# Query transposes moved ahead of the first up, three scans behind it, and three small sums moved later, in a fused linear-attention and SoLU kernel

## The chip, the cores and the metric

One core of a Trainium2 chip runs the whole program in one launch. The metric is the device time of one execution in microseconds (us); for the kernel before, the median of 3 runs is 367.84 (367.70 to 368.34). TensorE is called PE here, its weight loads PEld, VectorE DVE, ScalarE ACT, GpSimd POOL, and the engine that issues most of the transfers SP.

## What is computed

The reference, cut to what matters (4 batches, 8 heads, 768 steps, head width 48; 3072 tokens, model width 384, hidden width 1024; float32):

```python
state = zeros((B, H, D, D))
for t in range(S):
    state = alpha[:, :, t, :, None] * state + einsum('bhd,bhe->bhde', k[:, :, t], v[:, :, t])
    y[:, :, t] = einsum('bhd,bhde->bhe', q[:, :, t], state)
x = y.transpose(0, 2, 1, 3).reshape(B * S, H * D)
h = x @ w_in
solu = h * softmax(h)
ln = (solu - mean(solu)) / sqrt(var(solu) + 1e-6) * g_ln
return ln @ w_out
```

So each head carries a 48 by 48 state, decayed per row by alpha, and the attention's output goes through a hidden layer with a softmax gate and a layer norm.

## The kernel before, in words

**Tiling.** The 768 steps are cut into 6 groups of 128 steps; a group holds 128 steps of all 4 batches, 512 tokens, that is 4 output tiles of 128 tokens. Groups are counted from 0 in the code: g or a = 2 is the third. For each group there are two halves of work:

- *Attention.* Decays, keys and queries are turned so that the head's rows lie on partitions. `alpha_T` (L187) turns alpha by two DVE transposes (`firsts` L178, 128x1024, and `lasts` L181, 128x512). `scan_back` (L206) makes products of decays from each step to the group's end (`hT`), three parts; `inverses` (L211) takes a reciprocal; `scan_on` (L215) makes the products from the start (`aT`), again three parts of 128x516, part 2 for the last 16 rows of the heads and parts 0 and 1 for the first 32 rows. All six scans are DVE instructions of L204. `keys_T` and `keys` (L219, L223) turn the keys on DVE and multiply them on POOL (L225). `queries(i)` (L250, L253) multiplies part i of the queries by `aT` on POOL; `apart` (L243, L245, ACT) splits the last rows by parity. `scores` (L271, L278) multiplies keys and queries on PE into four banks, `masked` (L286, L289, DVE) takes them to `sT`; `read_state` and `read_values` (L348, L356, L333) make the output x; `next_state` (L365) carries the state. `move_lasts` and `move_firsts` (L227, L234) copy the queries within the on-chip memory by twelve transfers from SP's queue into `lot`, from which `decay` (L255, L261, POOL) and `read_state` read.
- *Hidden layer.* For each of 8 slices s of the hidden width, `up` (L386) makes h on PE (6 matmuls, L394) in one of two banks, ACT takes the exponent `e` (L408), DVE the product `room` (L409), ACT its square (L412). `room` frees the bank of h. `running` (L415, L427) adds the slices up in p, one half on POOL, one on DVE. `token_sums` (L454) adds up over partitions on PE (L462), transposes the result on DVE (L467) and makes from it, by three small DVE operations (L469, L471, L473), what `finish` needs. `down` (L501, L507) makes an output tile on PE, `finish` (L518) scales it: small DVE operations, a power on POOL (L546), ACT (L548), the transfer out (L549).

**Order.** The order on each engine is that of the code; nothing is rearranged. The first two groups' attention and the first group's hidden layer are written out by hand (L668 to L843). From L922 on a loop runs over groups g = 1 to 5, with steps s = 0 to 7: at each step comes one `up` of group g, and pieces of group g+1's attention are hung in by a table, `first` (L853) for g = 1 and `usual` (L847) for the others. Places of a step are, in order: head, up, behind, `running`, middle, `down`, tail. In `first`, step 1 has "on1" behind the up (one scan of the third group), step 2 "lasts firsts" (query transposes, POOL's products and the moves), step 3 `keys_back` at its head and "apart" behind, steps 4 and 5 the scores and masks. In `usual`, step 1 has all three scans. With g = 1 no `down` is in the loop's steps 0 to 6, so that PE goes from one up to the next.

By hand, in front of the loop, stand for the third group: `alpha_T(2)` (L818), `scan_back(2, .)` (L836), `inverses(2)`, `keys_T(2)`, `keys(2)`, the loads of alpha and keys of the fourth group (L834, L840) and `scan_on(2, 2)`, `scan_on(2, 0)` (L842, L843). The load of the fourth group's queries is issued by "firsts" in step 2 (L888), behind the moves in SP's queue. SP waits at each transfer that it issues until its sources and its target are free.

Of the kernel before, what the change touches and what calls it, by code (L numbers as in the profile page):

```python
# [9 lines left out]
FP = mybir.dt.float32  # L10
# [4 lines left out]
ALU = mybir.AluOpType  # L15
AX = mybir.AxisListType
P = 128
# [15 lines left out]
def fast_path(ctx, tc, q, k, v, alpha, moe_w_in, moe_w_out, moe_g_ln, out):  # L33
# [12 lines left out]
    nc = tc.nc  # L46
    B, H, S, D = q.shape
    NTOK, DM = out.shape
    DFF = moe_w_in.shape[1]
# [12 lines left out]
    def pool(name, bufs, **kw):  # L62
        return ctx.enter_context(tc.tile_pool(name=name, bufs=bufs, **kw))
# [4 lines left out]
    small = pool("small", 4)  # L68
# [31 lines left out]
    qn = const.tile([P, H, TQ, D], FP, name="qn")  # L100
# [20 lines left out]
    qv = const.tile([P, 2 * H, SW], FP, name="qv")  # L121
    qe = const.tile([P, NP, SW], FP, name="qe")
# [5 lines left out]
    gr = [dict() for _ in range(G)]  # L128


    def load(src, dst, g):
        t = slice(g * P, (g + 1) * P)
        for b in range(B):
            nc.sync.dma_start(
                out=dst[32 * b : 32 * b + 32].rearrange("t h u d -> t h (u d)"),
                in_=src[b, :, t, :].rearrange("h (t u) d -> t h (u d)", u=TQ),
            )
# [35 lines left out]
    def load_v(g):  # L173
        t = slice(g * P, (g + 1) * P)
        for b in range(B):
            nc.sync.dma_start(out=held(vn, b), in_=v[b, :, t, :].rearrange("h p d -> p h d"))

    def firsts(src, dst):  # L178
        nc.vector.transpose(out=dst.rearrange("p h (t u) -> p h u t", u=TQ), in_=src[:, :, :, 0:E0])  # L179

    def lasts(src, dst):  # L181
        nc.vector.transpose(
            out=dst.rearrange("p j (i t u) -> p u j i t", u=TQ, i=2),
            in_=src[:, :, :, E0:D].rearrange("p (j i) u d -> p u j i d", i=2),
        )
# [14 lines left out]
    def scan(out, data, start, flip):  # L200
        a, o, s = (x.rearrange("p j s -> p (j s)") for x in (data, out, start))
        if flip:
            a, o, s = a[:, ::-1], o[:, ::-1], s[:, ::-1]
        nc.vector.tensor_tensor_scan(out=o, data0=a, data1=s, initial=1.0, op0=ALU.mult, op1=ALU.add)  # L204
# [10 lines left out]
    def scan_on(g, i):  # L215
        part = slice(NP * i, NP * i + NP)
        scan(aT[:, part], aT[:, part], seed[:, part], False)

    def keys_T(g):  # L219
        firsts(kn, kT[:, 0:H])  # L220
        lasts(kn, kT[:, H:NB])
# [43 lines left out]
    def quarter(b):  # L265
        return slice(32 * b, 32 * b + 32)
# [19 lines left out]
    def masked(half, batches=range(B)):  # L286
        a = masks[half]
        for b in batches:
            nc.vector.tensor_tensor(  # L289
                out=sT[:, b, half * NP : half * NP + NP], in0=a[b], in1=mask[:, None, :].to_broadcast([P, NP, P]),  # L290
                op=ALU.mult,
            )
# [161 lines left out]
    def token_sums(g):  # L454


        d = gr[g]
        t = ps_a.tile([P, B, 2, 32], FP, tag="a3", name="rows") if g else ps_h.tile([P, B, 2, 32], FP, tag="h", name="rows")
        for b in range(B):
            for r in range(4):  # L460
                c = b * P + 32 * r
                nc.tensor.matmul(  # L462
                    t[quarter(r), b], lhsT=d["unit"][:, 0:32], rhs=d["p"][:, :, c : c + 32], start=True, stop=True,
                    tile_position=(0, 32 * r), skip_group_check=True,
                )
        tt = work.tile([P, B, 2, 32], FP, name="cols")
        nc.vector.transpose(out=tt.rearrange("p b i t -> p (b i t)"), in_=t.rearrange("p b i t -> p (b i t)"))  # L467
        s = sums[:, g * B : g * B + B]
        nc.vector.tensor_copy(out=s[:, :, 1:3], in_=tt[:, :, :, 0])  # L469
        sq = small.tile([P, B], FP, name="sq")  # L470
        nc.vector.tensor_tensor(out=sq, in0=s[:, :, 1], in1=s[:, :, 1], op=ALU.mult)  # L471
        d["s"] = small.tile([P, B], FP, name="s")
        nc.vector.scalar_tensor_tensor(  # L473
            out=d["s"], in0=sq, scalar=1e-6 * DFF, in1=s[:, :, 2], op0=ALU.mult, op1=ALU.add
        )

    def last_norm():

# [39 lines left out]
    def finish(n):  # L518
        g, b = divmod(n, B)
        d = st[n]  # L520
        s, whole = sums[:, n], d.get("held", d["o"])
        o = whole[:, 0:DM]
        t0 = b * S + g * P
        if g == G - 1:
            o_sb = work.tile([P, DM], FP, name="o_sb")
            r = gr[g]["r"][:, b : b + 1]
            nc.vector.tensor_scalar(out=o_sb[:, 0:P], in0=o[:, 0:P], scalar1=r, scalar2=None, op0=ALU.mult)  # L527
            nc.scalar.activation(out=o_sb[:, P:DM], in_=o[:, P:DM], func=AF.Copy, scale=r)  # L528
            nc.scalar.dma_start(out=out[t0 : t0 + P, :], in_=o_sb)
            d.clear()  # L530
            return
        nc.vector.tensor_copy(out=s[:, 0:1], in_=whole[:, DM : DM + 1])
        t = small.tile([P, 1], FP, name="t")
        nc.vector.scalar_tensor_tensor(
            out=t, in0=s[:, 0:1], scalar=-1.0 / DFF, in1=s[:, 0:1], op0=ALU.mult, op1=ALU.mult
        )
        nc.vector.tensor_tensor(out=s[:, 3:4], in0=t, in1=gr[g]["s"][:, b : b + 1], op=ALU.add)  # L537
        if g == 0:

            centred = work.tile([P, DM], FP, name="o_mean")  # L540
            nc.vector.scalar_tensor_tensor(
                out=centred, in0=mean_sb, scalar=s[:, 0:1], in1=o, op0=ALU.mult, op1=ALU.add
            )
            o = centred
        r = small.tile([P, 1], FP, name="r")
        nc.gpsimd.tensor_tensor(out=r, in0=s[:, 3:4], in1=mhalf, op=ALU.pow)  # L546
        o_sb = work.tile([P, DM], FP, name="o_sb")
        nc.scalar.activation(out=o_sb, in_=o, func=AF.Copy, scale=r)  # L548
        nc.sync.dma_start(out=out[t0 : t0 + P, :], in_=o_sb)  # L549
        d.clear()  # L550
# [166 lines left out]
    for i in (0, 2, 1):  # L717
        if i == 1:
# [3 lines left out]
            out=qe[:, :, 0:P] if i == 2 else qv[:, part, 0:P], in0=t[i], in1=aT[:, part, 1:SW], op=ALU.mult  # L722
# [98 lines left out]
    down(2, 1)  # L821
    scores(1, 1)
    masked(1)
    finish(0)
    finish(1)
    finish(2)
# [8 lines left out]
    for i in range(3):  # L835
# [3 lines left out]
    keys(2)  # L839
    load(k, kn, 3)  # L840
    down(3, 1, (2, 3))
    scan_on(2, 2)  # L842
    scan_on(2, 0)  # L843

# [6 lines left out]
    first = dict(  # L853
        head={3: "keys_back"},
        behind={
            0: "v", 1: "on1", 2: "lasts firsts", 3: "apart", 4: "scores0 masked0", 5: "scores1 masked1 decay",
            7: "alpha back",
        },
        tail={6: "begin read0"},
# [3 lines left out]
    def attend(a, what):  # L863

        more = a + 1 < G
        if what == "v":
            load_v(a)
        elif what == "keys":
            keys_T(a)
            keys(a)  # L870
            if more:
                load(k, kn, a + 1)
        elif what[:2] == "on":
            if what == "on2":
                inverses(a)
            scan_on(a, int(what[2]))
        elif what == "lasts":
            lasts(qn, qe[:, :, 0:P])
            ends_of_decay()
            queries(2)  # L880
            move_lasts()
        elif what == "firsts":
            firsts(qn, qv[:, 0:H, 0:P])
            queries(0)
            queries(1)
            move_firsts()
            if more:
                load(q, qn, a + 1)  # L888
        elif what == "apart":
            apart()  # L890
        elif what == "decay":
            decay(a)
        elif what == "keys_back":
            if more:
                keys_back(a)
        elif what[:6] == "scores":
            scores(a, int(what[6]))
        elif what[:6] == "masked":
            masked(int(what[6]))
        elif what == "alpha" and more:  # L900
            alpha_T(a + 1)
            if a > 2:
                attend(a, "over")
        elif what == "over" and more:
            alpha_over(a + 1)
            if a + 2 < G:
                load(alpha, an, a + 2)
        elif what == "back" and more:
            for i in range(3):
                scan_back(a + 1, i)  # L910
        elif what == "begin":
            read_begin()
        elif what[:4] == "read":
            read_state(int(what[4]))
        elif what == "values":
            read_values(a)
        elif what == "kv" and more and a != 4:
            next_state(a)
# [59 lines left out]
    def compare(out, x, bound, op):  # L978
# [6 lines left out]
        out=chunks[:, :, 2], in0=sums[:, :, 2], scalar=0.25, in1=sums[:, :, 3], op0=ALU.mult, op1=ALU.is_le  # L985
# [6 lines left out]
    else:  # L992
# [9 lines left out]
        out=bad, in0=all_ok[0:1, 0:1], scalar1=float(P * ends[-1]), scalar2=None, op0=ALU.is_lt  # L1002
# [451 lines left out]
```

## Time and profile before

| what | value |
|---|---|
| median of 3 runs | 367.84 us |
| the profiled execution's own time | 367.97 us |
| span of the profiled execution | 366.2 us |
| TensorE clock granted | 1.0 of full speed |
| DVE scans, L204 | 36, mean 1399 ns (`hT`) and 1551 ns (`aT`) |
| DVE transposes of the queries, 128x1024 and 128x512 | mean 2032 and 1107 ns |
| L469, L471, L473 on DVE | mean 172, 166 and 166 ns |
| POOL key product L225, 128x1024 | mean 2182 ns |
| POOL query products L253 | mean 1090 (`qe`) and 1240 ns (`qv`) |

The profile is of one execution. Its page gives busy time by engine and groups of instructions by line; the timeline gives the start and length of each instruction, counted from the span's start, with the idle time before it and what ended that; `out<-in` names the tiles. "x4" merges instructions in a row. Ends of matmuls are modelled, so lengths of PE's rows overlap the next row; starts don't. A wait is put down to what came last.

### The profile page before, as it was taken

The page shows a single profiled execution, that of the slowest core. Times are in us where ns is not written, and L with a number is a line of the kernel's source. Part 1 is how long each engine was busy: PE and PEld are TensorE (multiplying, and loading weights), DVE is VectorE, ACT ScalarE, POOL GpSimd, SP SyncE. Part 2 cuts the span into 40 slices and gives each one's busy share as a digit, 9 for nine tenths or more (in the row PEclk, how much of TensorE's full clock was granted, in tenths as well). Part 3 has the DMA queues.
Part 4 walks back from the last instruction along what each step waited for, and adds up shares of the span by engine and source line. Part 5 has one row for each costly group of instructions (what it writes and reads, how often), then busy time and mean ns, then how long its engine had stood idle before and what let it go on. Part 6 is the DMA issues. An engine that isn't in the chain of part 4 may idle for free. (4 is left out here: it accounts for less than half of the span.)

```text
span 366.2 us, 10036 instructions
## 1 busy us (share of the span) xinstructions
PE 357.8 (98%) x4341; PEld 215.0 (59%) x4341; DVE 245.0 (67%) x375; ACT 146.4 (40%) x260; POOL 132.2 (36%) x129
## 2 busy tenths in 40 slices
PE   8899999999999999999999999999999999999994
PEld 8784355666755566566575456475556565555552
DVE  0999989979998797936675935766946314345420
ACT  3647878182645262252521252431241132222110
POOL 7020000004449963774133764232773121233300
PEclk9999999999999999999999999999999999999999
DMA  9995995326196409463035354004041000000011
GB/s 180 183 338 152 204 309 124 88 67 159 50 234 141 109 21 180 85 152 94 21 92 112 83 121 126 3 25 88 21 107 55 0 25 0 24 21 22 23 47 51
DMA packets 72871, 36.06 MB, mean 98 GB/s; under 512 B 48232, under 2 KB 70000, under 8 KB 72816
## 3 DMA queue, kind: packets, MB, share of 16 engines
q1 hardware_dynamic: 71792, 34.39, 39.8%
q10 hardware_dynamic: 1024, 0.92, 0.8%
q8 instruction: 36, 0.59, 0.7%
q14 instruction: 19, 0.16, 0.2%
HBM read 25.30 MB, written 4.72 MB: 82 GB/s over the span
## 5 line engine op out<-in xcount | busy, mean ns | idle before, releaser
L507 PE MATMUL o<-w_out,room 128*128 128x385 f32 x384 | 134.0, 492 | 0.0
L394 PE MATMUL h<-x,w_in 128*128 128x512 f32 x288 | 131.7, 597 | 0.5 <-DVE g_col L642 0.5
L507 PEld LDWEIGHTS o<-w_out,room 128*128 128x128 f32 x384 | 71.0, 189 | 54.7 <-issue 13.1
L394 PEld LDWEIGHTS h<-x,w_in 128*128 128x128 f32 x288 | 53.2, 189 | 58.6 <-issue 48.5
L409 DVE TENSOR_TENSOR room<-h,e 128x512 f32<-128x512 f32 x40 | 27.5, 689 | 72.9 <-ACT e L408 72.9
L408 ACT ACTIVATE e<-h 128x512 f32<-128x512 f32 x40 | 24.0, 599 | 100.2 <-PE h L394 100.2
L427 POOL TENSOR_TENSOR p<-p,e 128x512 f32<-128x512 f32 x30 | 43.7, 1458 | 20.0 <-ACT e L408 19.9
L412 ACT ACTIVATE u<-room 128x512 f32<-128x512 f32 x40 | 25.2, 630 | 38.3 <-DVE room L409 38.3
L546 POOL TENSOR_TENSOR r<-sums,mhalf 128x1 f32<-128x1 f32 x20 | 14.8, 741 | 69.7 <-DVE sums L537 69.4
L289 DVE TENSOR_TENSOR sT<-a,mask 128x512 f32<-128x512 f32 x43 | 26.7, 681 | 8.0 <-PE a L278 7.9
L204 DVE TENSOR_TENSOR_SCAN hT<-aT,unit 128x516 f32<-128x516 f32 x18 | 24.4, 1399 | 7.6 <-ACT aT L703 7.5
L204 DVE TENSOR_TENSOR_SCAN aT<-aT,seed 128x516 f32<-128x516 f32 x18 | 27.4, 1551 | 0.2
L225 POOL TENSOR_TENSOR kT<-kT,hT 128x1024 f32<-128x1024 f32 (+1 forms) x8 | 14.2, 1800 | 32.7 <-DVE kT L179 32.7
L427 DVE TENSOR_TENSOR p<-p,u 128x512 f32<-128x512 f32 x30 | 22.5, 749 | 5.1 <-ACT u L412 5.1
L278 PEld LDWEIGHTS a<-qv,kT 32*128 32x128 f32 x704 | 21.4, 186 | 7.0 <-issue 2.6
L278 PE MATMUL a<-qv,kT 32*128 32x128 f32 x704 | 23.9, 278 | 0.4 <-POOL qv L253 0.3
L212 POOL COPY fend<-hT 128x12 f32<-128x12 f32 x6 | 3.1, 509 | 55.9 <-DVE hT L204 55.9
L333 PE MATMUL y<-sT,vn 128*32 128x128 f32 x768 | 22.6, 273 | 0.2 <-DVE sT L289 0.2
L333 PEld LDWEIGHTS y<-sT,vn 128*32 128x32 f32 x768 | 20.7, 110 | 1.6 <-issue 1.0
L196 ACT ACTIVATE sq<-an,mone 128x1536 uint8<-128x1536 f32 x12 | 18.9, 1572 | 0.2
L548 ACT ACTIVATE o_sb<-o,r 128x384 f32<-128x384 f32 x16 | 9.3, 582 | 18.5 <-POOL r L546 18.5
L261 POOL TENSOR_TENSOR state<-state,lot 128x384 f32<-128x384 f32 x10 | 8.8, 903 | 13.1 <-DMA lot<-qv 13.1
(148 smaller groups left out, 374.3 us busy)
## 6 DMA issues: line engine op xcount, KB each, us to landing
vn<-in_v_dram SPq DMA_DIRECT2D x24, 192.0 KB, 4.7
an<-in_alpha_dram SPq DMA_DIRECT2D x20, 192.0 KB, 4.1
out_dram<-o_sb SPq DMA_DIRECT2D x20, 192.0 KB, 1.9
room<-in_moe_w_out_dram SPq DMA_DIRECT2D x8, 384.0 KB, 5.5
kn<-in_k_dram SPq DMA_DIRECT2D x16, 192.0 KB, 5.6
qn<-in_q_dram SPq DMA_DIRECT2D x16, 192.0 KB, 4.1
lot<-qe SPq DMA_DIRECT2D x40, 64.5 KB, 2.1
lot<-qv SPq DMA_DIRECT2D x20, 129.0 KB, 2.4
```

Of the source, the lines that this page charges most:

```text
L196: nc.scalar.activation(out=sq, in_=x, func=AF.Relu, scale=sign, bias=mone, accum_out=over[:, g, i : i + 1])
L204: nc.vector.tensor_tensor_scan(out=o, data0=a, data1=s, initial=1.0, op0=ALU.mult, op1=ALU.add)
L278: nc.tensor.matmul(a[b][:, i], lhsT=kT[quarter(b), kb], rhs=qv[quarter(b), qb, 0:P], start=not last and not i, stop=bool(last), tile_posit ...
L289: nc.vector.tensor_tensor(out=sT[:, b, half * NP : half * NP + NP], in0=a[b], in1=mask[:, None, :].to_broadcast([P, NP, P]), op=ALU.mult,)
L333: nc.tensor.matmul(y_bank(b)[quarter(r), a], lhsT=lhsT, rhs=rhs, start=(b, r) not in begun, stop=stop, tile_position=(row, 32 * r), skip_g ...
L394: nc.tensor.matmul(h, lhsT=w_in[:, a, f * P : (f + 1) * P], rhs=d["x"][:, a].rearrange("p b t -> p (b t)"), start=(a == 0), stop=(a == KC ...
L408: nc.scalar.activation(out=e, in_=h, func=AF.Exp)
L409: nc.vector.tensor_tensor(out=u, in0=h, in1=e, op=ALU.mult)
L412: nc.scalar.activation(out=u2, in_=u, func=AF.Square)
L427: eng.tensor_tensor(out=p, in0=d[0][i] if f == 1 else p, in1=d[f][i], op=ALU.add)
L507: nc.tensor.matmul(d["o"][:, 0 : DM + 1], lhsT=u_of(g, f)[:, b * P : b * P + P], rhs=w_out[:, f], start=(f == 0), stop=(f == FC - 1), skip ...
L546: nc.gpsimd.tensor_tensor(out=r, in0=s[:, 3:4], in1=mhalf, op=ALU.pow)
```

## The change

Three things move; no instruction is added or removed.

- In `token_sums` the three small DVE operations behind the transpose become a function; for g = 0 it is kept and called by hand ahead of `finish(0)`, behind `masked(1)` of the second group. For the other groups it is called at once, as before.
- For the third group, the two query transposes (`lasts`, `firsts`) take the place of `scan_on(2, 2)` and `scan_on(2, 0)` in front of the loop, and the three scans stand together behind the second group's up of step 1 ("on2 on0 on1").
- The load of the fourth group's queries is issued right behind these transposes: in SP's queue it moves ahead of the fourth tile's output, of the third group's values and of the twelve moves.

```diff
         s = sums[:, g * B : g * B + B]
-        nc.vector.tensor_copy(out=s[:, :, 1:3], in_=tt[:, :, :, 0])
-        sq = small.tile([P, B], FP, name="sq")
-        nc.vector.tensor_tensor(out=sq, in0=s[:, :, 1], in1=s[:, :, 1], op=ALU.mult)
-        d["s"] = small.tile([P, B], FP, name="s")
-        nc.vector.scalar_tensor_tensor(
...
+        def rest():
+            nc.vector.tensor_copy(out=s[:, :, 1:3], in_=tt[:, :, :, 0])
...
+        if g:
+            rest()
+        else:
+            d["rest"] = rest
...
     masked(1)
+    gr[0]["rest"]()
     finish(0)
...
     down(3, 1, (2, 3))
-    scan_on(2, 2)
-    scan_on(2, 0)
+    lasts(qn, qe[:, :, 0:P])
+    firsts(qn, qv[:, 0:H, 0:P])
+    load(q, qn, 3)
...
-            0: "v", 1: "on1", 2: "lasts firsts", 3: "apart", 4: "scores0 masked0", 5: "scores1 masked1 decay",
+            0: "v", 1: "on2 on0 on1", 2: "lasts firsts", 3: "apart", 4: "scores0 masked0", 5: "scores1 masked1 decay",
...
-            if what == "on2":
+            if what == "on2" and a > 2:
                 inverses(a)
...
         elif what == "lasts":
-            lasts(qn, qe[:, :, 0:P])
+            if a > 2:
+                lasts(qn, qe[:, :, 0:P])
             ends_of_decay()
             queries(2)
             move_lasts()
         elif what == "firsts":
-            firsts(qn, qv[:, 0:H, 0:P])
+            if a > 2:
+                firsts(qn, qv[:, 0:H, 0:P])
             queries(0)
             queries(1)
             move_firsts()
-            if more:
+            if more and a > 2:
                 load(q, qn, a + 1)
```

More of the change, by code (lines that the diff above doesn't have):

```diff
@@ L468, in token_sums @@
         s = sums[:, g * B : g * B + B]
-        nc.vector.tensor_copy(out=s[:, :, 1:3], in_=tt[:, :, :, 0])
-        sq = small.tile([P, B], FP, name="sq")
-        nc.vector.tensor_tensor(out=sq, in0=s[:, :, 1], in1=s[:, :, 1], op=ALU.mult)
-        d["s"] = small.tile([P, B], FP, name="s")
-        nc.vector.scalar_tensor_tensor(
-            out=d["s"], in0=sq, scalar=1e-6 * DFF, in1=s[:, :, 2], op0=ALU.mult, op1=ALU.add
-        )
+        def rest():
+            nc.vector.tensor_copy(out=s[:, :, 1:3], in_=tt[:, :, :, 0])
+            sq = small.tile([P, B], FP, name="sq")
+            nc.vector.tensor_tensor(out=sq, in0=s[:, :, 1], in1=s[:, :, 1], op=ALU.mult)
+            d["s"] = small.tile([P, B], FP, name="s")
+            nc.vector.scalar_tensor_tensor(
+                out=d["s"], in0=sq, scalar=1e-6 * DFF, in1=s[:, :, 2], op0=ALU.mult, op1=ALU.add
+            )
+        if g:
+            rest()
+        else:
+            d["rest"] = rest
     def last_norm():
```

## The prediction

> **What bounds the kernel now.** I read the page first, then the waits of TensorE, then the timelines of all engines from 60 to 125 us, where the change acts. Times below are us from the span's start. The page:
>
> ```profile
> PE 357.8 (98%) x4341; PEld 215.0 (59%) x4341; DVE 245.0 (67%) x375; ACT 146.4 (40%) x260; POOL 132.2 (36%) x129
> ```
>
> TensorE (PE) is busy throughout, so a microsecond counts only if it opens or closes a hole in PE's stream. A busy share hides short holes, because ends of matmuls are modelled; I compare starts. A block of 64 score matmuls (L278) takes 2.00 from its start to the next block's in seven of the ten places after the first group. It is longer in three, all near the change. In the timeline of the weight loads:
>
> ```profile
> 77.87 0.29 PEld L278 LDWEIGHTS a<-qv,kT 32*128 32x128 f32 x2 [0.55 <-DVE aT L204]
> 78.50 1.87 PEld L278 LDWEIGHTS a<-qv,kT 32*128 32x128 f32 x62 [0.34 <-DVE qv L811]
> ```
>
> The second group's first scores start at 77.87 and hand over at 80.49: 2.62, so 0.62 are lost to the last query product on VectorE (DVE), which ends at 78.45. (The second bank of scores is the one that this product reads.) The other place, in PE's timeline:
>
> ```profile
> 107.55 5.32 PE L394 MATMUL h<-x,w_in 128*128 128x512 f32 x12
> 113.12 2.26 PE L278 MATMUL a<-qv,kT 32*128 32x128 f32 x64 [0.26 <-POOL qv L253]
> 115.32 2.84 PE L394 MATMUL h<-x,w_in 128*128 128x512 f32 x6
> ```
>
> Two ups take 5.57 here, from 107.55 to 113.12, against 5.25 for the pair at 100.99; the scores take 2.20, not 2.00. So 0.52 are lost to GpSimd's (POOL's) query product and, in the last matmuls, to ScalarE's (ACT's) `apart`, which ends at 114.61, 0.71 before the block does. After 123 no block is longer than its like. All holes near the change sum to 0.62 + 0.52 + 0.14 (second scores, 118.09) = 1.28.
>
> DVE around the second place:
>
> ```profile
> 97.56 2.61 DVE L204 TENSOR_TENSOR_SCAN aT<-aT,seed 128x516 f32<-128x516 f32 x1
> ...
> 102.18 0.66 DVE L409 TENSOR_TENSOR room<-h,e 128x512 f32<-128x512 f32 x1
> ...
> 105.08 0.69 DVE L409 TENSOR_TENSOR room<-h,e 128x512 f32<-128x512 f32 x1 [0.34 <-ACT e L408]
> 105.68 1.79 DVE L204 TENSOR_TENSOR_SCAN aT<-aT,seed 128x516 f32<-128x516 f32 x1
> 107.40 0.66 DVE L427 TENSOR_TENSOR p<-u,u 128x512 f32<-128x512 f32 x1
> 107.98 0.68 DVE L409 TENSOR_TENSOR room<-h,e 128x512 f32<-128x512 f32 x1
> 108.59 1.11 DVE L182 STREAM_TRANSPOSE qe<-qn 128x512 f32<-128x512 f32 x1
> 109.55 2.05 DVE L179 STREAM_TRANSPOSE qv<-qn 128x1024 f32<-128x1024 f32 x1
> ```
>
> The `room` rows are the steps s = 0, 1, 2; each frees one of two `h` banks, so PE's up of step s+2 waits for `room` of step s. Up 4 is the second half of the 107.55 row (from 110.17) and finds `room` 2 done at 108.66: cover of 1.5.
>
> **A rule and this trace.** The Trainium skill, "SBUF — State Buffer", section "SBUF: two separate sides", says that a DVE operation with two SBUF inputs and a GpSimd operation share a port pair as an exclusive lock: who starts first keeps it for the whole instruction, and the other blocks. The trace agrees:
>
> ```profile
> 96.91 2.18 POOL L225 TENSOR_TENSOR kT<-kT,hT 128x1024 f32<-128x1024 f32 x1 [2.22 <-DVE kT L179]
> 105.12 1.27 POOL L427 TENSOR_TENSOR p<-e 128x512 f32<-128x512 f32 x1 [1.21 <-ACT e L408]
> 147.58 2.23 POOL L427 TENSOR_TENSOR p<-e 128x512 f32<-128x512 f32 x1
> ```
>
> An undisturbed scan takes 1.23 (at 72.69). The one at 97.56 takes 2.61: it ends 1.09 after POOL's row of 96.91 does (99.09). The one at 105.68 ends 1.09 after POOL's 106.39. At 147.58 POOL is the loser: 2.23 for what takes 1.27. The forecast goes by this, turn by turn. Transposes have one input and don't block: 1.10 at 96.61, most of it under POOL's 2.18.
>
> **The change, part by part.**
>
> (a) Three small DVE operations (L469, L471, L473) leave the stretch ahead of the second group's transposes: 63.16 to 63.65, so 0.49. DVE has no gap from there to 78.45, hence the product ends at 77.96, and PE's hole falls from 0.62 to 0.13. PE and DVE are 0.49 earlier up to the end of `masked(1)` (87.50). There the three operations come back, and DVE's first `finish` starts at 88.02, as before. So DVE is where it was and PE 0.49 early.
>
> (b) Ahead of the second group's first up, two scans (97.56 to 102.18, 4.62, stretched by POOL's key products) give way to the two query transposes: 2.84 (82.81 to 85.63 for the same pair), so `room` 0 starts at 100.40. The gain of 1.78 isn't kept whole: `room` 1 needs h of up 1, which PE finishes at 103.12 (103.61 less 0.49). With ACT's lag `e` starts at about 103.25, and 0.61 later (104.47 to 105.08) `room` 1: 103.86, against 105.08.
>
> The order of the instructions on PE, ACT and POOL is the same in both kernels; only DVE's and SP's differ.
>
> (c) Behind `room` 1 there are now three scans instead of one, and they meet POOL. POOL's p takes 103.91 to 105.18; scan 2 waits for it and ends at 106.27 (+1.09); scan 0 goes next, to 107.40, and scan 1 to 108.52 (starts 0.08 under the end before, 1.21 each); POOL's two short copies sit behind scans. Now POOL's query product, waiting since 107.33, has its turn: 1.05 (the row of 147.58 ends 1.06 after the scan that held it), to 109.57. DVE's p goes after it, 0.55 (DVE's p of 113.41 ends 0.54 after POOL's product), to 110.12, and `room` 2 starts at **110.04**, where it was 107.98. The transposes no longer stand behind it, but that doesn't help the chain after it.
>
> (d) That chain is ScalarE's, in its order: `room` 2 to square 0.72 (107.98 to 108.70), square to the four copies of `keys_back` 0.53, to `e` of step 3 1.48 (109.23 to 110.71), to `room` 3 0.61, to its square 0.73 (112.02 to 112.75), to `apart` 0.53, `apart` 1.33, to the end of the scores 0.71. Sum 6.64: the scores end at 116.68, where they ended at 115.32: **+1.36**. On the way PE has a hole ahead of up 4 (ready at 109.68, bank free at 110.73), which lies inside this. POOL's products are done by then (second by 111.2), so its wait is gone; what is late next is `room` 2, and behind it `apart`. Step 4, `masked0` and the second scores follow rigidly (all hang on `apart` or on the scores), and nothing later has slack to give on PE. With both gains of 0.49 and the vanished POOL wait inside it, the whole is +1.36.
>
> (e) SP's queue: the loads of `qn` for the fourth group now stand ahead of the fourth tile's output, of `vn` and of the twelve `lot` moves. They wait for the transposes, done at 100.5, before SP comes to them. Nobody soon waits for that output or for `vn` (needed at 127.96). The transfer engines are full there (share 1.06 from 102.18 to 107.55, 0.90 to 113.12). Before, `vn` landed by 112.73 and the moves were issued from 110.90 to 119.98; four `qn` loads land about 0.85 apart (123.23 to 125.90), so `vn` is 3 later, and the issue of its four, which lasted to 110.02, too by some 1.5 to 2. The moves are then 1.5 to 2.05 late. The state's product on POOL (121.42, waiting for `lot`) had some 0.2 to spare before PE read it at 123.0. So this costs between nothing beside (d) and +1.85 in its place.
>
> The profiled execution took 367.97 with a span of 366.2; it is 0.13 over the median of 367.84. I add the change to the median: 367.84 + 1.36 = **369.2**.
>
> **Rivals.**
> 1. *The gain comes as meant* (ends faster). Place: the scores at 113.12. If `room` 2 starts early enough, PE loses neither there nor at 77.87: -0.49, -0.52, at most -0.14 more: 366.7. By (d) a start of `room` 2 after 108.68 costs and one before it gains; a gain over 0.74 needs 107.9. Three free scans from 104.46 (3.5) give about 108.6, so the ACT chain would have to be shorter too. 7%.
> 2. *The scans meet little of POOL*: three in 3.5 to 4.4 (4.43 in the fourth group, 146.39 to 150.82). `room` 2 at 108.6 to 109.6: 367.8 to 368.7. For it: in the fourth group only one scan in three was held. Against: here p starts ahead of the scans, and the products come inside. 21%.
> 3. *POOL takes one turn more* (its product ahead of scan 1, the next ahead of DVE's p): another 1.1, 370.3. The order is decided by 0.01 us. 12%.
> 4. *The transfers bind* (e): 369.7; with a further hold-up of the queue, as L237's last at 118.05 (1.93 instead of 0.59), 370.5. 16%.
>
> The forecast (368.6 to 369.6) has 44%.
>
> **Numbers.** About 0.2% (0.74 us) is what can be told from no change. Slower: forecast, rivals 3 and 4: 0.72. Same: rival 2 but for its lowest end, 0.20. Faster: rival 1 and that end, 0.08. The range of 8 in 10 takes in rival 2's lower end and most of rivals 3 and 4: 367.9 to 370.3; the likeliest case alone is 368.6 to 369.6.
>
> **What the changed profile would show.** (a) right: L278's block of 77.87 near 2.1, the blocks after it 0.5 earlier. (b): `room` 0 at 100.4, `room` 1 near 103.9. (c): POOL's query product and DVE's p stretched, `room` 2 near 110.0; if `room` 2 is at 108.7 or earlier, the forecast falls. (d): a hole of about 1 ahead of up 4, `apart` ending near 116.0. (e): `vn` landing near 115.6; the read of the state later than rigid would show rival 4.

## The result, and the profile after

| | before | after |
|---|---|---|
| median, us | 367.92 (367.70 to 368.47, 6 runs) | 370.13 (369.64 to 371.67, 6 runs) |
| ratio, 95% interval | | 1.0063 (1.0043 to 1.0082) |
| profiled execution, us (span) | 367.97 (366.2) | 370.23 (368.4) |

The changed kernel is slower, by 2.2 us where 1.36 were forecast. The time lies inside the range of 8 in 10 (367.9 to 370.3), near its upper end, and above the likeliest case (368.6 to 369.6). A second measurement of it on another chip (e11 below) gave 371.34, a ratio of 1.0077 (1.0061 to 1.0093), which lies above the range. So the direction and the place were right and the size was too small; this section and the experiments find the missing part.

The page of the changed kernel, first TensorE's (PE's) share and then its costliest group that waits (busy time, mean ns, then idle time ahead of it and what ended it):

```profile
PE 359.3 (98%) x4341; PEld 216.0 (59%) x4341; DVE 243.7 (66%) x375; ACT 146.2 (40%) x260; POOL 132.7 (36%) x129
L394 PE MATMUL h<-x,w_in 128*128 128x512 f32 x288 | 131.9, 597 | 1.5 <-DVE room L409 0.9
```

The share is again 98%, and PE's busy time grew by 1.5 without one matmul more, so the share says nothing of the place. What is new is the 0.9 us that an `up` waits for `room`. PE's timeline shows where:

```profile
78.51 2.07 PE L278 MATMUL a<-qv,kT 32*128 32x128 f32 x64
80.50 2.86 PE L513 MATMUL o<-w_out,room 128*128 128x385 f32 x8
...
107.53 2.74 PE L394 MATMUL h<-x,w_in 128*128 128x512 f32 x6
111.21 2.84 PE L394 MATMUL h<-x,w_in 128*128 128x512 f32 x6 [0.94 <-DVE room L409]
113.98 1.17 PE L278 MATMUL a<-qv,kT 32*128 32x128 f32 x32
115.88 1.34 PE L278 MATMUL a<-qv,kT 32*128 32x128 f32 x32 [0.72 <-ACT qv L245]
117.15 2.84 PE L394 MATMUL h<-x,w_in 128*128 128x512 f32 x6
...
124.83 1.40 PE L333 MATMUL y<-lot,state 64*32 64x128 f32 x64
```

The same block before:

```profile
123.00 1.16 PE L333 MATMUL y<-lot,state 64*32 64x128 f32 x64
```

The first scores take 1.99 from start to start: the hole of 0.62 at 77.87 is gone. Up to 107.5 PE stands where it stood before (107.55). Then comes the hole ahead of up 4, and a second one in the scores, behind `apart`. The third group's scores end at 117.15, before at 115.32: **+1.83**. The block that reads the state starts at 124.83 (before 123.00) and takes 1.34 instead of 1.09 to the next block's start: +0.25 more. From there on the two traces run nearly parallel: 2.07 apart here, 2.25 at the end of the span.

VectorE (DVE) in the changed kernel:

```profile
98.13 1.18 DVE L182 STREAM_TRANSPOSE qe<-qn 128x512 f32<-128x512 f32 x1
99.09 2.18 DVE L179 STREAM_TRANSPOSE qv<-qn 128x1024 f32<-128x1024 f32 x1
101.07 0.72 DVE L409 TENSOR_TENSOR room<-h,e 128x512 f32<-128x512 f32 x1
...
104.47 0.69 DVE L409 TENSOR_TENSOR room<-h,e 128x512 f32<-128x512 f32 x1 [0.78 <-ACT e L408]
105.08 4.04 DVE L204 TENSOR_TENSOR_SCAN aT<-aT,seed 128x516 f32<-128x516 f32 x3
109.05 1.51 DVE L427 TENSOR_TENSOR p<-u,u 128x512 f32<-128x512 f32 x1
110.48 0.68 DVE L409 TENSOR_TENSOR room<-h,e 128x512 f32<-128x512 f32 x1
```

`room` 1 waits for ScalarE's (ACT's) exponent. Behind it come the three scans in one stretch, then DVE's part of `p`, which takes 1.51 for what took 0.66 before, and only then `room` 2: 110.48, before 107.98. GpSimd (POOL) in the same stretch:

```profile
107.95 2.05 POOL L253 TENSOR_TENSOR qe<-qe,aT 128x512 f32<-128x512 f32 x1
...
123.52 1.64 POOL L261 TENSOR_TENSOR state<-state,lot 128x384 f32<-128x384 f32 x2 [4.34 <-DMA lot<-qv]
```

The first query product ends at 110.00, 0.88 after the last scan, and DVE's `p` at 110.56, 0.56 after that product: the two engines take turns, as in the trace of before. The last row is the state's product, which waited 4.34 for the moves into `lot`; before:

```profile
121.42 1.65 POOL L261 TENSOR_TENSOR state<-state,lot 128x384 f32<-128x384 f32 x2 [0.67 <-DMA lot<-qv]
```

SP's queue shows why; here a length is the time that the issue of the whole row took. The changed kernel, then two rows of before:

```profile
104.13 2.51 SPq L134 DMA_DIRECT2D qn<-in_q_dram  x4
...
108.11 5.70 SPq L176 DMA_DIRECT2D vn<-in_v_dram  x4
113.91 5.19 SPq L232 DMA_DIRECT2D lot<-qe  x8
119.19 2.94 SPq L237 DMA_DIRECT2D lot<-qv  x4
```

```profile
105.05 4.97 SPq L176 DMA_DIRECT2D vn<-in_v_dram  x4
110.90 5.17 SPq L232 DMA_DIRECT2D lot<-qe  x8
```

With the queries' load ahead of them, the values' load starts at 108.11 (before 105.05) and the moves at 113.91 (before 110.90): 3.0 late. The last move lands at 123.91, before at 121.74.

### The profile page after: what moved, and what is told of

Its sections match the earlier page's. It is cut to its first block, busy times and chain, and to the rows that moved or that the text cites. A ratio compares the mean times of both kernels' runs of the same rounds, so it can differ in the third digit from the quotient of the medians.

```text
span 368.4 us, 10037 instructions
## 1 busy us (share of the span) xinstructions
PE 359.3 (98%) x4341; PEld 216.0 (59%) x4341; DVE 243.7 (66%) x375; ACT 146.2 (40%) x260; POOL 132.7 (36%) x129
## 5 line engine op out<-in xcount | busy, mean ns | idle before, releaser
L225 POOL TENSOR_TENSOR kT<-kT,hT 128x1024 f32<-128x1024 f32 (+1 forms) x8 | 13.3, 1679 | 32.7 <-DVE kT L179 32.7
L204 DVE TENSOR_TENSOR_SCAN aT<-aT,seed 128x516 f32<-128x516 f32 x18 | 24.9, 1420 | 0.2
```

## The experiments

All runs below are compared with runs of the kernel before on the same chip, whose median was 368.3. The theory after the result: (1) the loss is the chain scans, POOL's turns, DVE's `p`, `room` 2, `apart`; (2) the load of `qn` adds a wait at the read of the state; (3) the sums' move is worth nothing. The rival to (1) is that only the number of scans behind up 1 counts; the rival to (3) is that its 0.5 comes through.

### What each of the three parts is worth

**e1_sums**: the kernel before with the first part of the change alone, the function in `token_sums` and its call:

```diff
...
     masked(1)
+    gr[0]["rest"]()
     finish(0)
```

> The kernel before with the three small sums moved alone. Theory (the third group's scores hang on DVE, which runs unbroken from the second group's masks to the third group's query transposes): the second group's first scores lose about 0.1 instead of 0.6, but the sums come back on DVE ahead of finish(0), so DVE's transposes of the third group's queries, POOL's product after them and the start of those scores stay where they were, and the time is that of before within 0.1 us. Rival (the hole's worth is kept): 0.5 us faster than before.

Measured: 368.53, ratio 1.0004 (0.9996 to 1.0012). The hole in the first scores is gone (78.03, 1.99 to the next block), and still nothing is gained. PE's timeline shows where the lead went:

```profile
91.32 3.70 PE L333 MATMUL y<-sT,vn 128*32 128x128 f32 x126
95.22 0.38 PE L333 MATMUL y<-sT,vn 128*32 128x128 f32 x2 [0.20 <-issue]
95.53 1.56 PE L513 MATMUL o<-w_out,room 128*128 128x385 f32 x4
```

PE reaches this block at 91.32, 0.47 ahead of before, and leaves it at 95.53, where before leaves it at 95.42: the block takes 4.21 instead of 3.63. The last two of its matmuls are held up with no semaphore that ends the wait ("issue"). In the records of the transfers a 16 KB instruction transfer ends 1.37 before the end of that stall (93.85, against 95.22). The same stands in the second trace of the changed kernel (93.72 and 95.16). In the trace of before the transfer ended at 93.56 and PE, later by itself, met no stall. Over all thirteen traces, PE leaves this block 1.57 to 1.75 after that transfer's end in the six where the block takes longer than 3.64, and 1.63 to 1.98 after it in the seven others. That PE waited for its instructions fits, but no run moved such a transfer by itself, so it isn't shown.

In e1 the lead would have gained nothing even without this stall, as its theory said. The three sums come back on DVE, so DVE is no earlier than before: `room` 0 is at 102.33 (before 102.18), `room` 1 at 105.22 (before 105.08), and the third group's scores wait for POOL's query product as before (0.28 and 0.26). With the transposes and scans turned it is otherwise: there `room` 1 waits, by way of `e`, for PE's h, and a lead of PE would count.

**e2_turn**: the changed kernel without the sums' move. **e3_load_back**: the changed kernel with the load back behind the moves. **e10_turn_load_back**: both, so the turn of transposes and scans alone. The edit of e3:

```diff
-    load(q, qn, 3)
...
-            if more and a > 2:
+            if more:
                 load(q, qn, a + 1)
```

> The changed kernel without the sums' move. Theory: the hole of 0.6 ahead of the second group's scores is there again, but the scans behind up 1 set the time: 1.9 to 2.4 us slower than before, equal to the changed kernel within 0.4. Rival (the sums' return on DVE is a good part of the loss): within 1.4 us of before.

> The changed kernel with the load of the fourth group's queries back behind the moves. Theory: the state's product on POOL no longer waits late for the moves; the first read of the state takes 1.1 instead of 1.34, so 0.2 to 0.4 us faster than the changed kernel. Rival (the load is the main cost): 1.5 us or more faster than the changed kernel, near before.

> The move of transposes and scans alone: no move of the three small sums, and the queries' load back behind the moves. Theory: with the load back the time is set by the chain behind room 2, and room 2 by the scans and GpSimd's turns, which start at room 1; room 1 comes from TensorE's h of up 1, so the 0.5 us hole in the first scores (no move of the sums) comes through: about 0.4 to 0.6 over the same kernel with the sums moved (ratio near 1.0055 to 1.006). Rival: VectorE's own stream up to the transposes bounds room 1, and the sums' move is worth nothing here either: ratio within 0.0006 of 1.0044.

**e11_changed_again**: the changed kernel once more.

> The changed kernel once more, on the chip of the other two, for its ratio and for how its start and its transfers differ from one execution to the next. Theory: ratio 1.005 to 1.007; a hole of 0.9 ahead of up 4, the scores 1.8 to 2.1 later than before, the read of the state with 0 to 0.5 of waiting. Rival: the wait at the read of the state varies by more than 0.5 between executions, and the ratio with it (up to 1.008, as without the sums' move).

Ratios to the kernel before:

| | load ahead | load behind the moves |
|---|---|---|
| sums moved | 1.0063 (1.0043 to 1.0082); again 1.0077 (1.0061 to 1.0093) | e3: 1.0044 (1.0028 to 1.0060) |
| sums not moved | e2: 1.0080 (1.0063 to 1.0097) | e10: 1.0049 (1.0033 to 1.0066) |

Read downwards, the sums' move changes nothing that can be told: in e10 my theory expected 1.0055 or more, and the measured 1.0049 is the rival's value, though its interval holds both. Read across, the load ahead costs 0.0019 to 0.0033, some 0.7 to 1.2 us. On one chip the five runs of e2 (370.82 to 372.13) and of e3 (369.50 to 370.87) overlap only at their ends, as do the six each of e11 (370.83 to 371.91) and e10 (369.67 to 370.90) on the other (each pair differs in the sums' move as well); so there is such a cost, but its size is known only roughly. It is more than I had expected from the first trace: e2 came out 3.0 above before and not 1.9 to 2.4, and e3 gained more than 0.2 to 0.4. What is left, the turn alone, costs 0.0049, 1.8 us. The load's cost lies at the read of the state; e11:

```profile
125.92 0.55 PE L333 MATMUL y<-lot,state 64*32 64x128 f32 x16 [0.94 <-POOL state L261]
126.72 1.02 PE L333 MATMUL y<-lot,state 64*32 64x128 f32 x48 [0.25 <-POOL state L261]
```

Here PE waits 1.19, as it does in the trace of e2, where the first profile of the same queue order shows 0.25; in e3 it doesn't wait. So in e11 the rival was right. The scores end at the same time in e11 (117.22) and in the first trace (117.15). What differs is SP: the four loads of `qn` are out at 107.73 in e11 and at 106.64 in the first trace, because SP waits longer for earlier transfers to land (2.0 in all for the loads of alpha, against 1.0). The values and the moves are issued about 1 later, and the last move lands at 125.39 instead of 123.91. So this wait is between 0.25 and 1.2 in the traces taken, as the queue happens to run.

### What holds room 2

**e8_p_late**: as e3, with DVE's part of the first running sum moved behind `room` 2, and POOL's left in place.

```diff
-                running(g, s)
+                if g == 1 and s == 2:
+                    running(g, 1, (1,))
+                running(g, s, (0,) if g == 1 and s == 1 else (0, 1))
```

> The changed kernel with the query load back and with DVE's half of p of step 1 behind room 2 instead of ahead of it. Theory (p waits 0.8 for POOL's query product, which holds the port, and room 2 waits for p in DVE's order): room 2 starts 1.4 earlier, the hole ahead of up 4 nearly closes and the scores end 1.4 earlier; 1.2 to 1.5 us faster than e3_load_back. Rival (room 2 is not what the chain hangs on): equal to e3_load_back.

Measured: 368.20, ratio 1.0003 (0.9992 to 1.0014), 1.9 below e3, more than the 1.2 to 1.5 expected. DVE:

```profile
104.65 4.04 DVE L204 TENSOR_TENSOR_SCAN aT<-aT,seed 128x516 f32<-128x516 f32 x3
108.62 0.66 DVE L409 TENSOR_TENSOR room<-h,e 128x512 f32<-128x512 f32 x1
109.20 0.93 DVE L428 TENSOR_TENSOR p<-u,u 128x512 f32<-128x512 f32 x1
```

The three scans take the same 4.04, but `room` 2 starts right behind them, and the hole ahead of up 4 is gone. (`room`, which reads h from PSUM, needs no turn here: it takes its usual 0.66 inside POOL's row of 107.52 to 109.58. `p`, with both inputs in SBUF, took 1.51 against the same product in e3.) The 1.43 that `room` 2 spent behind `p` are what separates a loss from none. The number of scans behind up 1 is the same, so the rival to (1) falls. The scans aren't free by themselves, though: in this trace the scores still take 2.93, with 0.49 of waiting for `apart`, and end at 115.27, no earlier than before, although PE kept its lead of 0.5.

**e7_keys_back**: as e3, with the four copies of `keys_back` one step earlier, at the head of step 2, which takes them out of ACT's chain behind `room` 2.

```diff
-        head={3: "keys_back"},
+        head={2: "keys_back"},
```

> The changed kernel with the query load back and the turning of the keys one step earlier; all three scans stay behind up 1. Theory: the hole ahead of up 4 stays (room 2 is where it was), but the chain from room 2 to apart is shorter by up to 1.48, of which PE lets about 0.8 to 1.2 through: that much faster than e3_load_back. Rival (the copies are not in the chain): equal to e3_load_back.

Measured: 368.94, ratio 1.0022 (1.0015 to 1.0029), 1.1 below e3 (20 runs from 368.39 to 369.98; the execution traced took 368.44). The hole ahead of up 4 stays (0.95), but the scores that follow take 2.32 instead of 3.17. So more than half of e3's loss (1.1 of 1.7) runs through ACT's chain; the rest fits the bank that `room` 2 frees.

**e4_split**: the changed kernel with one of the three scans moved behind up 2. **e5_split_back**: the same with the load back behind the moves. **e6_split_back_keys**: e5 with `keys_back` at the head of step 2.

```diff
-            0: "v", 1: "on2 on0 on1", 2: "lasts firsts", 3: "apart", 4: "scores0 masked0", 5: "scores1 masked1 decay",
+            0: "v", 1: "on2 on0", 2: "on1 lasts firsts", 3: "apart", 4: "scores0 masked0", 5: "scores1 masked1 decay",
```

> The changed kernel with the scan of part 1 behind up 2 instead of up 1, so that one scan fewer stands ahead of room 2. Theory: room 2 starts 1.5 to 2.0 earlier, near 108.5, the hole ahead of up 4 is gone, and the scores end about 1.5 earlier; but the moves into lot, late because of the query load, then set the read of the state, so only 0 to 0.4 us of it arrive at the end. Rival (scans alone bind, the transfers don't): 1.4 us or more faster than the changed kernel. Second rival (the scans are not the cost): room 2 earlier but the scores end as late as before.

> The changed kernel with both edits: the scan of part 1 behind up 2, and the query load back behind the moves. Theory (two limits stand one behind the other, first the scans ahead of room 2 and then the moves that the load delays): the scores end near 114.8 as with the split alone, the state's product on POOL is done by 122, no hole ahead of the read of the state and no slow clock after it; 0.3 to 0.7 us faster than before, 2.3 to 2.8 faster than the changed kernel. Rival (the split costs something of its own): 1 us or more slower than before, as the split alone.

> The kernel of e5_split_back with the turning of the keys one step earlier (head of step 2 instead of 3), so that ScalarE's four copies no longer stand between the square of step 2 and e of step 3. Theory (the chain over ScalarE to apart sets the end of the scores): apart ends earlier, the scores take 2.0 instead of 2.5, 0.3 to 0.6 us faster than e5_split_back, 0.7 to 1.2 faster than before. Rival (DVE's room 3 behind the scan and p sets apart): no gain over e5_split_back.

e4 was a plain miss: 373.89 (371.24 to 375.72), ratio 1.0141 (1.0108 to 1.0174). On DVE it did what it should: `room` 2 at 108.04, no hole ahead of up 4, the scores over at 114.79. But PE, 2.4 earlier than in the changed kernel, then met the moves, which were no earlier (the last landed at 124.64):

```profile
125.13 0.55 PE L333 MATMUL y<-lot,state 64*32 64x128 f32 x16 [2.59 <-POOL state L261]
126.38 1.64 PE L333 MATMUL y<-lot,state 64*32 64x128 f32 x48 [0.69 <-POOL state L261]
127.94 5.20 PE L394 MATMUL h<-x,w_in 128*128 128x512 f32 x6
```

Two waits sum to 3.28, and the up behind them takes 5.20 instead of 2.84. In the view by stretches the granted clock is 0.97 from 124 to 126, 0.50 up to 132, and 0.82 to 134: half speed for 6.8 us. So the wait cost 3.3 and its effect on the clock over 2 more. The six runs say the same: the one with a mean granted clock of 1.0 took 371.24, the five with 0.989 to 0.993 took 372.71 to 375.72.

e5 shows that these were the moves' doing: 367.96, ratio 0.9994 (0.9985 to 1.0002), no wait at the read of the state, the scores over at 114.70. That is the gain in the place where it was expected, 0.62 earlier than before (115.32); the median keeps 0.3 of it, which the interval doesn't tell from none. What is left is that the scores take 2.48 and not 2.0, behind `apart`, behind `room` 3 at 111.42, behind `p` of step 2, which takes 1.51 in turn with POOL's products. e6 then gained nothing, 368.04, ratio 0.9996 (0.9988 to 1.0004), as its rival said: without the copies the exponent of step 3 is ready at 110.80, but `room` 3 stands behind the same `p` until 111.82.

### A version that beats both

**e9_best**: e6 with DVE's part of the running sum of step 2 behind `room` 3.

```diff
-                running(g, s)
+                if g == 1 and s == 3:
+                    running(g, 2, (1,))
+                running(g, s, (0,) if g == 1 and s == 2 else (0, 1))
```

> The split with the load put back and the copies of keys at the head of step 2, and VectorE's running sum of step 2 moved behind the room of step 3 (so that this room no longer waits behind a sum that is itself held by GpSimd's query product). Theory: the chain room 3 to square to apart sets the end of the third group's scores. Room 3 then starts when its exponent is there, near 110.8 instead of 111.8; the parity split ends near 113.4 instead of 114.3, the block of scores takes 2.0 to 2.1 instead of 2.5, and the time is 0.4 to 0.5 us below the split's 367.96: about 367.5, ratio to the kernel before 0.9985 to 0.999. Rival: the second half of GpSimd's query product becomes the last arrival, as in the kernel before (it ended at 112.8, at the start of the scores), and the gain is 0 to 0.2: ratio 0.9992 to 1.0.

Measured: 367.61 (367.34 to 368.16, 10 runs), before 368.33 on this chip, ratio 0.9972 (0.9959 to 0.9985): faster than the kernel before, by the medians 0.72 us.

```profile
108.44 0.68 DVE L409 TENSOR_TENSOR room<-h,e 128x512 f32<-128x512 f32 x1
...
110.92 0.69 DVE L409 TENSOR_TENSOR room<-h,e 128x512 f32<-128x512 f32 x1 [0.37 <-ACT e L408]
```

`room` 3 now waits for its exponent and not for POOL. PE:

```profile
112.70 2.07 PE L278 MATMUL a<-qv,kT 32*128 32x128 f32 x64
114.70 2.84 PE L394 MATMUL h<-x,w_in 128*128 128x512 f32 x6
```

The third group's first scores take 2.00 and the second group's too (78.17 to 80.17), so the two larger holes of the kernel before are closed. The small one in the third group's second scores isn't: they take 2.27, before 2.14.

## Why the prediction was right in direction and too small

- **(a) The sums.** The first half held: with the sums away the first scores have no hole (1.99, here and in e1). The step that failed is "PE 0.49 early". In the first trace PE lost this lead before it had it: TensorE's clock was granted in full from 7.25 instead of 4.71, DVE's first scan, which waits, by way of ACT, for what PE turns, started at 9.17 instead of 8.64, and PE came to the scores at 78.51 instead of 77.87. In e1 and e11, which came to these scores within 0.16 of before, it was early by 0.5 and lost it at 95, in the stall shown above. So in neither trace of the changed kernel did the lead reach `room` 1. Traces of e4, e5 and e7 kept the lead past 95, so it is not always lost; but e10 against e3 shows nothing of it in the median.
- **(b) The transposes.** `room` 0 at 101.07 (forecast 100.40) and `room` 1 at 104.47 (103.86). DVE came to `finish(0)` 0.65 late from the same late start, and the pair of transposes took 2.94 where 2.84 were put in. The 0.61 of `room` 1 is larger than the lead that (a) had promised: without it, h of up 1 comes at 103.61 and `room` 1 would be at 104.35, and 104.47 is what was seen.
- **(c) The turns.** Right, step by step: from `room` 1 to `room` 2 6.18 were worked out and 6.01 measured. The three scans in 4.04, POOL's product behind them, DVE's `p` behind that. The Trainium skill's rule in "SBUF — State Buffer" (section "SBUF: two separate sides") gave the turns, and durations of the trace of before gave their sizes. e8 showed that the turn of `p` is the one that decides.
- **(d) ACT's chain.** 6.64 from `room` 2 to the end of the scores were worked out, 6.67 measured, with the hole ahead of up 4 (0.94) inside. Since `room` 2 came 0.44 late by (a) and (b), the loss here is 1.83 and not 1.36. The turn alone without (a)'s lead would have been forecast at 1.36 + 0.49 = 1.85; e10 measured 1.8 (1.2 to 2.4 by its interval).
- **(e) SP's queue.** The moves were taken as 1.5 to 2.05 late, in place of (d) or hidden by it. They were 3.0 late at their first issue and 2.2 (first trace) to 3.65 (e11) at the last landing, and cost 0.25 to 1.2 on top of (d). The step that failed: the four loads of `qn` themselves wait in SP's queue for earlier loads, and all that stands behind waits as well. The third and fourth load of `qn` are issued at 105.47 and 106.33, right after the third and fourth load of alpha, eight transfers ahead of them, have landed (105.46 and 106.31); in e11 the same pairs are 106.46 and 107.42, after 106.44 and 107.40. The forecast had SP wait for the transposes only. The tolerance of 0.2 + 1.83 at the state's product was used up. Rival 4 is thus part of the truth, with a mechanism that adds to the forecast's.

The sum of 1.36 + 0.47 + 0.25 = 2.08 is the first trace's shift of the state's read by the end of it (2.07). Rival 1 (the gain as meant) falls with the three scans' 4.04 and `p`'s 1.51. Rival 2 (the scans meet little of POOL) had 3.5 to 4.4 for the scans, which holds; it falls with `p`'s 1.51, for `room` 2 came at 110.48 and not by 109.6. Rival 3 (one turn more) falls with `room` 2 less than half a microsecond from the forecast. That the first measurement still lies in the range is owed to the room that it left for rivals 3 and 4, and not to the sum, which took the lead of (a) as kept and (e) as hidden. Why PE stalls at 95 in some traces and not in others stays open.

## What to carry to other kernels

When a scan is moved next to another engine's products, count the turns on the shared port, and look at what stands between the last turn and the operation that frees a PSUM bank: putting that operation ahead of the sum that must wait its turn was worth 1.9 us here, nearly as much as moving a whole scan away (2.1). A load that is issued early pushes everything behind it in its queue; its price appears at the last transfer that someone waits for, and grows when the engines get faster. A microsecond that a hole gives back is only gained if it is still there at the next pinch, so follow it through the trace.

## What the runs showed of the hardware

- In e4 PE was idle from 122.5 but for 16 short matmuls (0.55 us), and then had half its clock from 125.9 to 132.7, 6.8 us, although it was busy from 126.4 on. The Trainium skill, "TensorE: Matmul & The Clock Gate", section "Part 1: The HAM clock gate (the "warmup" mystery)", tells of free-running windows of about 3.4 us, an idle one halving the clock and a busy one restoring it. The traces agree: every stretch of full clock in the thirteen traces is a whole number of 3.413 us (35 to 107 of them), and the 6.83 of half clock are two. They add that 0.55 us of matmuls in a stretch of 3.4 didn't keep the clock.
- The full clock at the start came at 4.02 to 7.25 us in the thirteen traces, though PE's first matmul starts at 1.08 in all; this spread of 3.23 is a little less than 3.413. In the first trace (7.25) PE was 0.63 behind before (4.71) at 29 us, and this was still there at 78: enough to hide a gain of 0.5 between two single profiles. In e3 (7.24) PE was 0.51 behind at 29, in e1 (6.48) only 0.15.
- PE can stall for about 0.5 us without any semaphore (95.2 in e1 and e11), 1.3 to 1.4 after an instruction transfer ends. The traces of e3 and e10 show the same at 35.9 and 35.4, 1.28 and 1.51 after such a transfer.
